# Attention and feed-forward on one core: 32-bit back transposes, a residual added by DMA, and a fifth shift tile

## The chip, the cores and the metric

The kernel runs on one core of one Trainium2 chip. The metric is the device time of one launch in microseconds (us), the median over runs. Engines are named as the profile names them: PE is TensorE (PEld its weight loads), DVE is VectorE, ACT is ScalarE, POOL is GpSimd, and SP is SyncE, which here only issues DMAs. PSUM has eight banks of 128 partitions by 512 fp32 numbers; matmuls write there, and ACT and DVE read it.

## The reference, cut to what matters

```python
x = A_x                                   # 2048 x 512, bf16
xn = _layernorm(x)
q = (xn @ wq) as 32 heads of 16;  k = xn @ wk;  v = xn @ wv     # one k and v for all heads
p = softmax(q k^T * 16 ** -0.5);  o = p v;  s = o @ wo
g = silu(silu(xn @ w1) @ w2)              # w1 512 x 1792, w2 1792 x 512
out = x + s * g
```

The exponentials are the largest part: 32 heads by 2048 queries by 2048 keys, which is 2048 tiles of 128 by 512.

## The kernel before, in words

**Units and groups.** The attention is cut into 32 groups of 64 units. A unit is one PSUM bank of scores (128 x 512), written by four 64x32 matmuls (`score`: L967 with a weight load, L961 where the weights that are loaded serve a second time). Its exponential is made in one of two ways. As a unit of kind A it goes to ACT, which takes one bank or two neighbouring banks in one instruction (`act_step`, L1674), and then into one product with the values. As a unit of kind D it goes to DVE, which in one pass (`pass_d`, L1042) writes an integer approximation of the exponential into `db_sb`; when a batch of eight such units is complete, POOL makes three shifted copies of it (`split`, L1225, `int64_add` on 4096 columns into a tile of `ds_sb`), and all four copies are multiplied with values of different weight and summed. So a D unit costs one DVE pass, three eighths of a POOL shift, and four products with the values where an A unit has one. Products with the values are line L1303 (`do_pv`).

**PE lanes.** Most matmuls are 64x32 tiles of the array. Four of them make up one half of the array, and two such halves, called lanes, run side by side: scores on lane 1, products with the values on lane 0, and the dense products (`product`, L705) on both.

**The rest of the work.** The layer norm runs ahead on DVE; `xn_sb` holds four normalised tiles, which PE transposes. For each quarter of the rows, `mk_h` and `mk_z` make the two feed-forward products; ACT and DVE apply the gates (`gated`, L761 and L762), and the gated result of a tile waits in `tmp_sb`. When a group is done (`make_norm`), DVE transposes its bank in 32x32 blocks (L1320), takes reciprocals (L1323) and multiplies into `otr_sb` (L1325); for every second group it transposes `otr_sb` back into `on_sb` (L1335), 512 bf16 columns. `mk_w` multiplies `on_sb` with wo for tiles 0 to 11; `final` then takes two DVE passes, bank times 0.25 times `tmp_sb` back into the bank (L814), and bank plus `xr_sb`, the reloaded x, into `ob_sb` (L817), which SP stores (L809). The last four tiles have a tail of their own (L1514 onward).

**The order.** Nothing is scheduled at run time. A planner in the file lays all operations out in a planned time, with a cost for each operation, and writes one fixed order per engine; each engine then runs its order and waits on semaphores. At each step PE's planner chooses between an A and a D unit by comparing the planned backlogs of ACT and of DVE:

```python
if a is not None and (d is None or ab < bl + mix.SLACK + mix.noise()):
```

so work moves between ACT and DVE until both are equally late. Thresholds such as `MARGIN` (a D batch is begun in a group only while at least so many of its units are unassigned) are drawn anew every 6000 planned ns from a list of seeds. The functions that the change and the prediction touch are these, as they stand before:

```python
NPA, NDB, NDS, NTM = 27, 3, 4, 4
MARGIN, MARGIN_END = 17, 20
...
def pick_d(t):
    if st["assigned"] < 8 or any(k not in evac_kt or evac_kt[k].op is None for k in range(NKT)):
        return None
```

The four tiles of `ds_sb` also hold x while it is normalised, in their last two; the first two are free for shifts from the start. The wait of `pick_d` is for the keys of all 16 tiles. POOL and DVE instructions that are marked `ports=2` are kept apart in the plan (`avail`).

Of the kernel before, what the change touches and what calls it, by code (L numbers as in the profile page):

```python
# [15 lines left out]
P = 128  # L16
# [6 lines left out]
SEEDS, STRETCH = [0, 0, 882634, 0, 348373, 328499, 78780, 554384, 89101, 903077, 320169, 0, 878569, 280070, 102111, 381856, 427096, 265022, 0, 740569, 0, 0, 0, 191854, 393933, 374197, 266972, 0, 665170, 0, 882882, 218695, 9227, 955074, 159633, 731624, 518155, 138034, 620799, 357599, 376984, 365473, 457970, 796664, 668429, 641664, 991272, 0, 0, 23990, 593814, 88565, 504692, 394759, 276845, 267858, 882770, 104810, 721623, 135503, 603776, 0, 337714, 100793, 638616, 0, 419715, 752789, 751312, 664693, 308960, 0, 762547, 276261, 218757, 897693, 0, 624478, 290921, 0, 713781, 335568, 417921, 100939, 814701, 0, 180062, 99721, 614963, 258262, 411291, 131548, 802432, 314922, 883804, 569039, 54637, 401726, 110613, 0, 983842, 914345, 0, 0, 0, 0, 0, 0, 0, 0], 6000.0  # L23
# [32 lines left out]
NPA, NDB, NDS, NTM = 27, 3, 4, 4  # L56
MARGIN, MARGIN_END = 17, 20
# [10 lines left out]
MATE = 176.663  # L68
RH, EVR, SC_PRIO, PES = 0, (0, 2, 3), 0, (1, 0)
# [6 lines left out]
class Task:  # L76
    __slots__ = ("eng", "dur", "emit", "reads", "writes", "prio", "preds", "op", "on_place", "dma", "gate", "ports", "after", "ring", "first")

    def __init__(self, eng, dur, emit, reads=(), writes=(), prio=5, preds=(), on_place=None, dma=0, gate=None, ports=1):
        self.ports, self.after, self.ring = ports, None, None  # L80
# [15 lines left out]
class Planner:  # L96

    def __init__(self):
# [7 lines left out]
        self.held = None  # L106
# [3 lines left out]
        self.last2 = {DV: None, PO: None}  # L110

# [68 lines left out]
    def tensor(self, mode, lane, dur, emit, reads, writes, t, after=None, n=8, held=None):  # L180
# [18 lines left out]
        if both or lane == 1:  # L199
            self.held = held  # L200
# [18 lines left out]
    def avail(self, task):  # L219
# [5 lines left out]
        if task.eng == PO and task.ports == 2:  # L225
            for d in self.tasks[DV]:
                if d.ports == 2 and d.gate is None and all(p.op is not None for p in d.preds) and (
                        self.ready(DV, d.reads, d.writes) <= self.clk[PO] + HOLD_PO):
                    return None
# [25 lines left out]
    def finalize(self, new_sem):  # L255
# [40 lines left out]
        for e in ENGINES:  # L296
            n = 0
            for op in self.order[e]:
# [5 lines left out]
                elif op.dma:  # L304
                    op.sem, op.val = new_sem(f"d{nd}"), 16
                    nd += 1
                elif op.inc:
                    n += 1
                    op.sem, op.val = sems[e], n

# [41 lines left out]
def bass_recurrent_scan__grouped_kv_mqa__dense_activation_silu__prompt_kernel(  # L352
# [29 lines left out]
    with ExitStack() as es:  # L382
# [25 lines left out]
        tmp_sb = sb("tmp_sb", [P, NTM, D], BF16)  # L408
        fin_sb = sb("fin_sb", [P, 2, D], BF16)
        ob_sb = sb("ob_sb", [P, 4, D], BF16)  # L410
        xr_sb = sb("xr_sb", [P, 4, D], BF16)
# [15 lines left out]
        pa3 = pa_sb[:].rearrange("p (b n) -> p b n", n=NQ)  # L427
        XB = NDS - 16 // BS
# [6 lines left out]

        pl = Planner()
        mix = Mix(A_HIGH=A_HIGH, D_HIGH=D_HIGH, SLACK=SLACK, MATE=MATE, HOLD=HOLD, PRESS=PRESS, PAIR_WAIT=PAIR_WAIT, STARVED=STARVED, SKIP=SKIP, J_SLIP=J_SLIP, START_H=START_H, START_Z=START_Z, JLATE=JLATE, NEXT_OB=NEXT_OB, OB_SLACK=OB_SLACK, MARGIN=MARGIN)
# [4 lines left out]
        xv = xf.rearrange("(t p) d -> p t d", p=P)  # L442

# [53 lines left out]
        pl.add(Task(PO, 1800.0, lambda g: g.memset(kt_sb[0:DH, 1, :], 0.0), [("xn", 3)], [("kt1", c) for c in range(NC)], 3,  # L497
                    gate=lambda: all(xn_task[t].op is not None for t in range(4)), ports=2))
        q1_fill = {}
        for r in range(NQR):  # L500
            q1_fill[r] = pl.add(Task(PO, T_MS, lambda g, r=r: g.memset(qt_sb[:, r, 1, :], 0.0), (), [("q1", r), ("qT", r, 1)], 2, ports=2,  # L501
# [1281 lines left out]
```

## Time and profile before

| | before |
|---|---|
| median of 3 runs | 658.18 us (658.02 to 658.38) |
| span of the profiled execution, first to last instruction | 656.6 us |
| its device time outside the span, by the median | 1.6 us |
| busy: PE, ACT, DVE, POOL | 648.1, 640.4, 639.3, 571.0 us |
| instructions | 44475 |
| granted TensorE clock | 1.000 |

The profiled execution has no time of its own beside its span, so the median stands for it. Busy time counts an engine that works on anything; PE's is no measure of its rate, since its matmuls overlap. In the groups of instructions the mean duration of one instruction is longer than the step from one to the next, since the start of one overlaps the end of the one before; where a step matters it is read from the timeline.

### The profile page before, as it was taken

To read this page: it belongs to the slowest core of one execution; us is meant where nothing else is said; L and a number is where in the kernel's file an instruction comes from. 1 tells how busy PE (TensorE), PEld (TensorE's weight loads), DVE (VectorE), ACT (ScalarE), POOL (GpSimd) and SP (SyncE) were. 2 spreads that over 40 slices of the span, in tenths; PEclk is the share of its full clock that TensorE was granted. 3 is DMA by queue.
4 is the path that set the end of the run, shared out by engine and by line. 5 is a ranking of instruction groups with operands and counts; after the bars stand their busy time and mean duration, and the time that the engine had idled before them with its cause. 6 is when DMAs were issued, how large, how long until landed. Compare 5 with 4: busy or idle time off the path is not lost.

```text
span 656.6 us, 44475 instructions
## 1 busy us (share of the span) xinstructions
PE 648.1 (99%) x22180; PEld 330.7 (50%) x19436; DVE 639.3 (97%) x1170; ACT 640.4 (98%) x1128; POOL 571.0 (87%) x320
## 2 busy tenths in 40 slices
PE   8999999999999999999999999999999999999997
PEld 4445554544455554554555454444555555554444
DVE  8999999999999999999999999999999999999976
ACT  6889999999999999999999999999999999999995
POOL 4038899999998978999999878999999999889991
PEclk9999999999999999999999999999999999999999
DMA  6311111000011100000000010000000000100001
GB/s 177 129 48 42 42 28 29 10 4 10 5 35 28 35 28 4 10 4 6 9 4 12 20 36 26 4 5 9 5 10 4 10 21 20 35 11 5 4 4 34
DMA packets 13641, 15.92 MB, mean 24 GB/s; under 512 B 2320, under 2 KB 12816, under 8 KB 13456
## 3 DMA queue, kind: packets, MB, share of 16 engines
q1 hardware_dynamic: 12976, 12.36, 6.3%
q8 instruction: 162, 2.65, 1.7%
q0 software_dynamic: 192, 0.46, 0.2%
q10 hardware_dynamic: 288, 0.26, 0.1%
q14 instruction: 23, 0.19, 0.1%
HBM read 8.95 MB, written 2.10 MB: 17 GB/s over the span
## 4 chain that ended last, share of the span: by engine, by line
PE 84%; ACT 10%; DVE 3%; POOL 1%; DMA 0%; issue 0%
PE ps L967 28%; PE ps L1303 23%; PE ps L705 20%; PE ps L961 13%; ACT pa_sb L1674 9%; ACT t_sb L761 1%; DVE stats_sb L539 1%; DVE xn_sb L568 1%; PE ps L1514 1%; DVE xnT_sb L618 0%; DMA kt_sb<-kt_sb 0%; POOL qt_sb L501 0%; POOL kt_sb L497 0%; DVE v_sb L679 0%; DVE kt_sb L651 0%
## 5 line engine op out<-in xcount | busy, mean ns | idle before, releaser
L1674 ACT ACTIVATE pa_sb<-ps 128x512 bf16<-128x512 f32 (+1 forms) x1038 | 611.0, 771 | 4.1 <-PE ps L967 3.8
L1225 POOL INT64_ADD ds_sb<-db_sb x300 | 562.1, 1896 | 41.5 <-DVE db_sb L1042 31.9
L1042 DVE TENSOR_SCALAR db_sb<-ps 128x512 uint16<-128x512 f32 x808 | 499.9, 680 | 4.2 <-PE ps L961 2.0
L967 PE MATMUL ps<-qt_sb,kt_sb 64*32 64x512 bf16 x5448 | 470.6, 378 | 1.5 <-DVE v_sb L679 0.8
L1303 PE MATMUL ps<-ds_sb,v_sb 64*32 64x512 bf16 x4848 | 350.5, 377 | 0.0
L1303 PE MATMUL ps<-pa_sb,v_sb 64*32 64x512 bf16 x2480 | 269.9, 377 | 0.5 <-DVE v_sb L679 0.5
L961 PE MATMUL ps<-qt_sb,kt_sb 64*32 64x512 bf16 x2744 | 263.6, 375 | 0.0
L967 PEld LDWEIGHTS ps<-qt_sb,kt_sb 64*32 64x32 bf16 x5448 | 130.4, 89 | 162.8 <-ACT pa_sb L1674 70.6
L1303 PE MATMUL ps<-db_sb,v_sb 64*32 64x512 bf16 x1616 | 210.6, 377 | 0.0
L1303 PEld LDWEIGHTS ps<-ds_sb,v_sb 64*32 64x32 bf16 x4848 | 133.4, 91 | 43.5 <-issue 15.0
L705 PE MATMUL ps<-xnT_sb,w_sb 64*32 64x512 bf16 x1792 | 134.6, 377 | 0.0
L705 PE MATMUL ps<-w_sb,u_sb 64*32 64x512 bf16 x1792 | 133.5, 376 | 0.0
L1303 PEld LDWEIGHTS ps<-pa_sb,v_sb 64*32 64x32 bf16 x2480 | 91.4, 91 | 26.8 <-issue 7.9
L1303 PEld LDWEIGHTS ps<-db_sb,v_sb 64*32 64x32 bf16 x1616 | 66.5, 91 | 15.7 <-issue 5.3
L705 PEld LDWEIGHTS ps<-xnT_sb,w_sb 64*32 64x32 bf16 x1792 | 42.8, 91 | 24.9 <-issue 6.7
L705 PEld LDWEIGHTS ps<-w_sb,u_sb 64*32 64x32 bf16 x1792 | 44.4, 91 | 20.3 <-issue 6.2
L761 ACT ACTIVATE t_sb<-ps 128x512 bf16<-128x512 f32 x72 | 49.1, 682 | 0.0
L762 DVE SCALAR_TENSOR_TENSOR u_sb<-t_sb,ps 128x512 bf16<-128x512 bf16 x56 | 37.9, 677 | 1.0 <-ACT t_sb L761 1.0
L705 PE MATMUL ps<-xnT_sb,wq_sb 64*32 64x512 bf16 x480 | 37.1, 377 | 0.0
L705 PE MATMUL ps<-wo_sb,on_sb 64*32 64x512 bf16 x384 | 30.2, 377 | 0.0
L1320 DVE STREAM_TRANSPOSE ps<-ps 128x512 f32<-128x512 f32 (+1 forms) x33 | 23.2, 706 | 3.6 <-PE ps L1303 3.6
L1349 POOL DMA_DIRECT2D kt_sb<-kt_sb x4 | 2.3, 566 | 21.3 <-DVE rstd_sb L559 7.8
(78 smaller groups left out, 193.0 us busy)
## 6 DMA issues: line engine op xcount, KB each, us to landing
xr_sb<-in_A_x_dram SPq DMA_DIRECT2D x16, 128.0 KB, 2.4
out_dram<-ob_sb SPq DMA_DIRECT2D x16, 128.0 KB, 1.8
w_sb<-in_B_w_dram SPq DMA_DIRECT2D x1, 1792.0 KB, 7.3
w_sb<-in_B_w_dram SPq DMA_DIRECT2D x14, 128.0 KB, 2.1
ds_sb<-in_A_x_dram SPq DMA_DIRECT2D x3, 512.0 KB, 7.1
qt_sb<-qt_sb SPq DMA_DIRECT2D x16, 96.0 KB, 2.2
wq_sb<-in_A_wq_dram SPq DMA_DIRECT2D x1, 512.0 KB, 5.4
wo_sb<-in_A_wo_dram SPq DMA_DIRECT2D x4, 128.0 KB, 2.9
```

The lines of the kernel that those rows point to most:

```text
L539: ts_ = pl.add(Task(DV, 593.0, lambda v, t=t: v.bn_stats(stats_sb[:, t, :], x_tile(t)), [xkey(t)], [("st", t)], 1 + j, gate=(lambda j=j: S ...
L568: xn_task[i] = pl.add(Task(DV, 323.0, lambda v, i=i: v.tensor_scalar(xn_sb[:, i % 4, :], x_tile(i), mv_sb[:, i, 0:1], rstd_sb[:, i:i + 1], ...
L705: h = pe.matmul(bank(b)[32 * j:32 * (j + 1), :], lhsT=lhs(k, rows, 32 * j, 32), rhs=rhs(k, rows), start=first, stop=last, tile_position=(r ...
L761: t1 = Task(AC, T_AF + 0.8333 * NQ, lambda a: a.activation(t_sb[:, k, :], bank(b), ACT.Tanh, scale=scale), [("ps", b)], [("t", k)], 0)
L762: t2 = Task(DV, T_P, lambda v: v.scalar_tensor_tensor(out=dst, in0=t_sb[:, k, :], scalar=1.0, in1=bank(b), op0=ALU.add, op1=ALU.mult), [(" ...
L961: h = pe.add_instruction(mybir.InstMatmult(name=pe.bass.get_next_instruction_name(), engine=mybir.EngineType.PE, ins=[pe.lower_ap(q), pe.l ...
L967: h = pe.matmul(to, lhsT=keys, rhs=q, start=True, stop=True, tile_position=(r0, 32 * j), skip_group_check=True)
L1042: bt.P[k] = pl.add(Task(DV, T_P, lambda v: v.tensor_scalar(db_sb[:, bt.b, k * NQ:(k + 1) * NQ], bank(b), 128.0 * LOG2E, 128.0 * (SHIFT_BET ...
L1225: whole["po"].append(pl.add(Task(PO, T_P64, lambda g: g.int64_add(ds_sb[:, s, :].bitcast(U64), db_sb[:, bt.b, :].bitcast(U64), words), rea ...
L1303: h = pe.matmul(bank(OB)[q:q + 32, :], lhsT=lhs[rows], rhs=rhs[rows], start=s0, stop=s1, tile_position=(64 * l, q), skip_group_check=True)
L1320: t1 = pl.add(Task(DV, (T_TR - 60.0) / parts + 60.0, lambda v, cols=cols: v.transpose(bank(OB)[:, cols], bank(OB)[:, cols]), [("ps", OB)], ...
L1674: op = pl.place(AC, 0.8333 * NQ * n + T_AF, lambda a: a.activation(pa3[:, k0:k1 + 1:max(1, k1 - k0), :], ps3[:, b0:b1 + 1:step, :], ACT.Ex ...
```

## The change

**Back transposes on 32-bit units.** `otr_sb` is written with two 32-column blocks interleaved, and the transpose into `on_sb` reads pairs of bf16 as one 32-bit word: 256 words in place of 512 elements. `on_sb` then holds the queries of a block pair alternately, and its readers take every second column.

```diff
+        def on_cols(slot, rows, q, n):
+            if not TR32:
+                return on_sb[rows, slot, q:q + n]
+            b = q // 64 * 64 + q % 64 // 32
+            return on_sb[rows, slot, b:b + 63:2]
...
+                    return v.tensor_tensor(
+                        o4[:, pairs, :, DH * e:DH * e + DH], f3[:, bl, 0:DH].rearrange("p (b s) d -> p b s d", s=2),
+                        rcp_sb[:, e, bl].rearrange("p (b s) -> p b s", s=2).unsqueeze(3).to_broadcast([P, nb // 2, 2, DH]), ALU.mult)
...
+                    on_sb[:, oi % NON, cols].bitcast(FP32), otr_sb[:, oi % 2, cols].bitcast(FP32)) if TR32 else v.transpose(
...
-            product(jb, lambda k, rows, a, n: on_sb[rows, (NOC * c + k) % NON, r * P + a:r * P + a + n],
+            product(jb, lambda k, rows, a, n: on_cols((NOC * c + k) % NON, rows, r * P + a, n),
```

**Residual of tiles 0 to 11 by accumulating DMAs.** SP copies each x tile into the output in DRAM during the second quarter. `final` is one DVE pass into `ob_sb`, and POOL issues a DMA that adds `ob_sb` to the output.

```diff
         def final(tt, b):
-            k = tt % 2
+            if tt < NT - 4:
+                t1 = Task(DV, T_P, lambda v: v.scalar_tensor_tensor(
+                    out=ob_sb[:, tt % 4, :], in0=bank(b), scalar=0.25, in1=tmp_sb[:, tt % NTM, :], op0=ALU.mult, op1=ALU.mult),
+                    [("ps", b), ("xn", tt % NTM)], [("ob", tt % 4)], 0, [tmp_task[tt], out_task.get(tt - 4)])
+                fin_task[tt] = t1
+                out_task[tt] = pl.add(Task(PO, T_SWDGE, lambda e: e.dma_start(ov[:, tt, :], ob_sb[:, tt % 4, :], accum_op=ALU.add),
+                                           [("ob", tt % 4)], [("out", tt)], 0, [t1, xr_task[tt]], dma=256 * 1024, on_place=outs.append))
+                return t1,
...
+            if tt < NT - 4:
+                xr_task[tt] = pl.add(Task(SP, 60.0, lambda e: e.dma_start(ov[:, tt, :], xv[:, tt, :]),
+                                          (), [("out", tt)], 2, [], dma=256 * 1024))
+                later(xr_task[tt], hidden(1, tt))
+                return
```

**Buffers.** `tmp_sb` becomes another name of `xn_sb`; the tail's x, `fin_sb` and a new `fx_sb` lie in w1's memory, written after w1's last reader. The memory that is freed holds a fifth shift tile, so that three are free from the start.

```diff
-NPA, NDB, NDS, NTM = 27, 3, 4, 4
-MARGIN, MARGIN_END = 17, 20
+NPA, NDB, NDS, NTM = 27, 3, 5, 4
+MARGIN, MARGIN_END = 24, 20
...
+        tmp_sb = xn_sb
+        late = w1_sb[:].rearrange("p c f -> p (c f)")[:, 0:10 * D].rearrange("p (k n) -> p k n", n=D)
+        xr_sb, fin_sb, fx_sb = late[:, 0:4, :], late[:, 4:6, :], late[:, 6:10, :]
```

**Thresholds and order.** D units may start when the keys of 12 tiles are there, behind the layer norm's own passes; two waiting D passes in neighbouring banks are made in one instruction; POOL's two-port instructions also wait for DVE's gated ones; and the list of seeds is another, so that the whole order is laid out anew. Further parameters come in with values that leave them without effect (products with the values on lane 1, zero fills and transposes by DMA).

```diff
+DPAIR, JA, JD = 25.0, 9000.0, 9000.0
+TR32, XBAR, T_TURN = 1, 0, 500.0
+YIELD, W_LATE = 1, 0.0
+DK, PRO_PRIO, ZDMA = 12, 6, 0
...
-            if st["assigned"] < 8 or any(k not in evac_kt or evac_kt[k].op is None for k in range(NKT)):
+            if st["assigned"] < 8 or any(k not in evac_kt or evac_kt[k].op is None for k in range(DK)):
...
-                op0=ALU.mult, op1=ALU.add), [("ps", b)], [("Db", bt.b, k)], 0, on_place=placed))
+                op0=ALU.mult, op1=ALU.add), [("ps", b)], [("Db", bt.b, k)], lambda: 0 if x_free[0] else PRO_PRIO, on_place=placed))
+            bt.P[k].slot = (b, bt.b * BS + k)
...
+        def both_passes(t, one):
+            for two in pl.tasks[DV]:
...
+                r = pl.avail(two)
+                if r is None or r > t + mix.DPAIR:
+                    continue
+                (b0, k0), (b1, k1) = sorted((one.slot, two.slot))
+                if k0 > k1 or b1 != b0 + 1:
+                    continue
...
+                op = pl.place(DV, one.dur + NQ / 0.96, lambda v: v.tensor_scalar(
+                    db3[:, k0:k1 + 1:k1 - k0, :], ps3[:, b0:b1 + 1:b1 - b0, :], 128.0 * LOG2E, 128.0 * (SHIFT_BETA + 127.0),
```

More of the change, by code (lines that the diff above doesn't have):

```diff
@@ L198, in tensor @@
         op.lane, op.n = lane, n
-        if both or lane == 1:
-            self.held = held
+        for i in range(2):
+            if both or i == lane:
+                self.helds[i] = held
         for i in range(2):
@@ L1305, in emit @@
                 return h
-            pl.tensor("U", 0, MM, emit, sorted(reads, key=str), [("ps", OB)], t, n=4 * len(mm))
+            last = ob_last.get(g)
+            ob_last[g] = pl.tensor("U", lane, MM, emit, sorted(reads, key=str), [("ps", OB)], t, n=4 * len(mm),
+                                   after=last if last is not None and last.lane != lane else None)
             make_shifts()
```

213 lines of the change are left out of this document (147 added, 66 removed).

## The prediction

> **What bounds the kernel now.** I read the page first (who is busy), then the windows between the first and the last shift on POOL (who is never idle), then the waits, and last the timeline for the step of each operation.
>
> ```profile
> PE 648.1 (99%) x22180; PEld 330.7 (50%) x19436; DVE 639.3 (97%) x1170; ACT 640.4 (98%) x1128; POOL 571.0 (87%) x320
> ```
> ```profile
> 0.00:44.80 44.80, 40.43 (x968) 19.35 (x882) 39.74 (x137) 35.74 (x63) 8.95 (x21) 1.00 0.41 128
> 44.80:642.70 597.90, 597.78 (x21000) 306.33 (x18352) 591.17 (x1017) 597.80 (x1057) 562.05 (x300) 1.00 0.06 16
> 642.70:656.60 13.90, 9.86 (x240) 4.98 (x212) 8.36 (x18) 6.84 (x11) 0.00 (x0) 1.00 0.12 40
> ```
> ```profile
> 625.48 0.39 PE L967 MATMUL ps<-qt_sb,kt_sb 64*32 64x512 bf16 x4
> ...
> 626.12 0.39 PE L967 MATMUL ps<-qt_sb,kt_sb 64*32 64x512 bf16 x4
> ```
> ```profile
> PEld ps L967 <- ACT pa_sb L1674: 70.6, 292, 0.5
> PEld ps L967 <- DVE db_sb L1042: 35.7, 165, 0.4
> POOL ds_sb L1225 <- DVE db_sb L1042: 31.9, 25, 5.7
> ...
> PEld ps L1303 <- POOL ds_sb L1225: 2.3, 8, 0.4
> ```
>
> The columns of the windows are length, PE, PEld, DVE, ACT, POOL. In the 597.9 us of the middle ACT is idle for 0.1 us and DVE for 6.7. PE's busy time says nothing, its count does: three score steps lie 0.64 us apart, so a lane makes four matmuls in 0.213 us and both lanes eight. The 21000 matmuls need 21000 / 8 x 0.213 = 559 us, so PE has 39 us to spare. POOL is idle for 35.9 us and mostly waits for DVE. The waits agree: the scores' weight loads stand 70.6 + 35.7 = 106 us for a bank that ACT or DVE still reads, and next to nothing waits for POOL. So ACT and DVE bound the middle together, and since the planner moves units between them, work taken off DVE is shared: a unit moved from A to D costs DVE one pass and saves ACT one exponential.
>
> ```profile
> L1674 ACT ACTIVATE pa_sb<-ps 128x512 bf16<-128x512 f32 x836 | 446.2, 694 | 2.6 <-PE ps L967 2.4
> L1674 ACT ACTIVATE pa_sb<-ps 128x1024 bf16<-128x1024 f32 x202 | 213.7, 1090 | 1.5 <-PE ps L967 1.4
> L817 DVE TENSOR_TENSOR ob_sb<-ps,xr_sb 128x512 bf16<-128x512 f32 x12 | 8.1, 677 | 0.0
> L814 DVE SCALAR_TENSOR_TENSOR ps<-ps,tmp_sb 128x512 f32<-128x512 f32 x12 | 8.2, 686 | 0.0
> L803 DVE SCALAR_TENSOR_TENSOR fin_sb<-ps,tmp_sb 128x512 bf16<-128x512 f32 x1 | 0.7, 692 | 1.1 <-PE ps L591 1.1
> L1335 DVE STREAM_TRANSPOSE on_sb<-otr_sb 128x512 bf16<-128x512 bf16 x15 | 10.5, 702 | 0.0
> L1320 DVE STREAM_TRANSPOSE ps<-ps 128x512 f32<-128x512 f32 x31 | 22.4, 723 | 2.1 <-PE ps L1303 2.1
> L1320 DVE STREAM_TRANSPOSE ps<-ps 128x256 f32<-128x256 f32 x2 | 0.8, 444 | 1.5 <-PE ps L1303 1.5
> L1325 DVE TENSOR_TENSOR otr_sb<-ps,rcp_sb 128x256 bf16<-128x256 f32 x31 | 12.7, 409 | 0.0
> L1325 DVE TENSOR_TENSOR otr_sb<-ps,rcp_sb 128x128 bf16<-128x128 f32 x2 | 0.4, 263 | 0.0
> L1349 POOL DMA_DIRECT2D kt_sb<-kt_sb x4 | 2.3, 566 | 21.3 <-DVE rstd_sb L559 7.8 <-DVE kt_sb L651 7.4 <-DVE mv_sb L543 6.1
> L705 PEld LDWEIGHTS ps<-wo_sb,on_sb 64*32 64x32 bf16 x384 | 8.9, 91 | 6.5 <-DVE db_sb L1042 1.4 <-issue 1.1 <-PE ps L705 0.7
> ```
> ```profile
> 39.20 3.67 DVE L1042 TENSOR_SCALAR db_sb<-ps 128x512 uint16<-128x512 f32 x6
> ...
> 74.58 0.70 DVE L1335 STREAM_TRANSPOSE on_sb<-otr_sb 128x512 bf16<-128x512 bf16 x1
> 75.21 2.45 DVE L1042 TENSOR_SCALAR db_sb<-ps 128x512 uint16<-128x512 f32 x4
> ...
> 208.44 0.67 DVE L817 TENSOR_TENSOR ob_sb<-ps,xr_sb 128x512 bf16<-128x512 f32 x1
> 209.03 0.24 DVE L1323 RECIPROCAL rcp_sb<-ps 128x16 f32<-128x16 f32 x1
> ...
> 649.26 0.76 DVE L1335 STREAM_TRANSPOSE on_sb<-otr_sb 128x256 bf16<-128x256 bf16 x2
> ```
> ```profile
> 47.63 0.49 ACT t_sb L761
> ```
>
> **The residual.** Twelve passes L817 go, none comes for them. In the timeline it starts at 208.44 and the next instruction at 209.03: a step of 0.59 us, and 12 x 0.59 = 7.1 us off DVE. The other pass now writes bf16 into SBUF where it wrote fp32 into PSUM: the same form in the tail (L803) lasts 692 ns against 686, so nothing. POOL gains twelve DMA issues. An accumulating DMA isn't in this trace; the nearest row is POOL's plain DMA (566 ns), and the next is a shift, 562.05 / 300 = 1.87 us. I take 0.57, the same kind of instruction, 6.8 us in all, hidden in POOL's 35.9 us of idle time. If POOL had no room, each microsecond more on it would come back as moved units, which is the rival on POOL below. The new wait: POOL waits for `final`'s pass, with the next shifts queued behind it, and PE's products behind those; the plan puts the issue where the pass has ended, and 2.3 us of PE's waits on POOL are the present scale.
>
> ```profile
> SPq L715 <- DVE qt_sb L723: 260.5, 14, 40.2
> ```
> ```profile
> DMA  6311111000011100000000010000000000100001
> ```
>
> SP loses twelve stores and keeps twelve x transfers, now from DRAM to DRAM. SP runs in order and stands up to 40 us before a move of queries, but these transfers have no consumer except the accumulation, and the moves that are queued behind them wait for DVE, not for SP. The DMA engines are busy for one or two tenths of a slice after the opening. `final` waits for the accumulation four tiles earlier to leave its buffer, a quarter of the kernel before. Zero for all three.
>
> **The back transposes.** Now 512 elements in 702 ns, with a step of 75.21 - 74.58 = 0.63 us. 32-bit transposes are in the trace at L1320: 512 words take 723 ns, the same as 512 short elements, and 256 words take 444. So the count sets the time, and the saving is 0.702 - 0.444 = 0.26 us, 15 x 0.26 = 3.9 us off DVE. The two halves in the tail (0.76 us together) lose the time of 128 elements each; by L1320's slope, (723 - 444) / 256 = 1.09 ns, that is 0.14 us each, and they lie in the tail's chain: 0.2 us off the end, since part of the second overlaps. The price: L1325 now writes every second bf16. Its slope is (409 - 263) / 128 = 1.14 ns an element. If a scattered write ran at half rate, 31 x 256 x 1.14 = 9.0 us would come onto DVE; below nothing it can't go, as the count stays. No row has a scattered write of this kind. [...] PE's weight loads of `on_sb` read every second column; the row now is 91 ns and overlaps the matmuls, and PE has its 39 us. Zero, and at double duration 384 x 91 ns / 4 = 8.7 us, still inside them (four loads run together).
>
> **Paired passes.**
>
> ```profile
> L1042 DVE TENSOR_SCALAR db_sb<-ps 128x512 uint16<-128x512 f32 x808 | 499.9, 680 | 4.2 <-PE ps L961 2.0 <-PE ps L967 1.1 <-POOL ds_sb L1225 0.2
> L651 DVE TENSOR_SCALAR kt_sb<-ps,part_sb 128x512 bf16<-128x512 f32 x3 | 2.2, 731 | 0.0
> L651 DVE TENSOR_SCALAR kt_sb<-ps,part_sb 128x384 bf16<-128x384 f32 x1 | 0.6, 600 | 0.0
> ```
>
> Six passes in a row take 3.67 us, the last of them its full 0.68, so the step of a pass is (3.67 - 0.68) / 5 = 0.60 us. A second bank in one instruction adds its 512 elements, 0.56 us by L1320's slope and 0.52 by L651's, (731 - 600) / 128 = 1.02 ns. So a pair saves 0.04 to 0.08; I take 0.06. How many? ACT, whose planner looks for neighbours, has 202 pairs. DVE's planner takes only those that happen to be ready within 25 ns, in neighbouring banks, in the right order, while PE stands 35.7 us for banks of DVE, so scores start one by one as banks come free. I take 20, between 0 and 135 (ACT's share, 404 of 1240 units, of some 820), 1.2 us. [...]
>
> **The sum for the middle.** DVE loses 7.1 + 3.9 + 1.2 = 12.2 us. A moved unit costs DVE 0.60 us and saves ACT 0.49 (the chain's step of one bank). Both end together when 12.2 - 0.60 n = 0.49 n, so n = 11.2 units and the gain is 5.5 us. What those units bring: 11.2 x 3 more products of two matmuls, 67 matmuls, 1.8 us of PE's 39; 11.2 x 3/8 = 4.2 shifts, 7.9 us of POOL. With the issues POOL takes 14.7 us more, and its room is 35.9 - 5.5 = 30.4. Both are covered. If no unit moved, ACT would still end where it does and the gain would be nothing: that is the lower bound.
>
> **The opening, the fifth tile, the rest.** Before 44.8 us ACT idles 9.1 us and DVE 5.1. D units may start with 12 tiles' keys, and three shift tiles stand free, but DVE has the layer norm to finish, and passes go behind it. If three or four of them fit in DVE's gaps, 2.1 us x 0.49 / 1.09 = 1.0 us; the bounds are 0 and 2.3 (all 5.1 us). The fifth tile and the higher `MARGIN` give POOL more room, where nothing waits: zero.
>
> ```profile
> L568 DVE TENSOR_SCALAR xn_sb<-ds_sb,mv_sb,rstd_sb x16: 403/408/415, 7.2 to 33.8; 128x512 bf16<-128x512 bf16 x16
> L762 DVE SCALAR_TENSOR_TENSOR tmp_sb<-t_sb,ps x16: 629/679/689, 119.3 to 634.2; 128x512 bf16<-128x512 bf16 x16
> L705 PE MATMUL ps<-xnT_sb,w_sb x1792: 373/376/388, 26.0 to 567.4; 64*32 64x512 bf16 x200
> L1514 PE MATMUL ps<-wo_sb,on_sb x96: 376/376/387, 645.4 to 650.1; 64*32 64x512 bf16 x96
> ```
>
> The columns here are shortest, median and longest duration, and first and last start. `xn_sb` is written last at 33.8 us and takes its new tenant at 119.3; w1 is read last at 567.4, and the tail's products with wo, which come before its x is needed, start at 645.4. So the shared buffers add waits that are over before they begin: zero. A newly drawn order may be a little better or worse everywhere; no row prices that, and I give it 2 us to either side, about the ends of the opening's bounds.
>
> Span: 656.6 - 5.5 - 0.2 - 1.0 = 649.9. The median lies 1.6 us above the profiled span, so 651.5 us.
>
> **The rivals.**
> - *More than the balance.* The opening is filled better (half of ACT's 9.1 us: 4.5 x 0.60 / 1.09 = 2.5, in place of 1.0) and pairs are as frequent as ACT's, 135 (115 more x 0.06 x 0.45 = 3.1). 646.9 us. For it: ACT's idle time is there. Against: DVE is the late one in the opening.
> - *The scattered write costs.* L1325 at half rate gives 9.0 of the 12.2 us back: 3.2 x 0.45 = 1.4 in place of 5.5, so 655.6 us. For it: no row excludes it. [...]
> - *Slower: pairs hold banks.* A pair frees its first bank 0.52 us later than a single pass, and PE already waits for DVE's banks 165 times in 808 passes. If each pair stops the score lane that long, and the other lane goes on, half of it counts: at 200 pairs 200 x 0.26 = 52 us, of which PE has 39 - 1.8 = 37 to spare; 15 are left, less 180 x 0.06 x 0.45 = 4.9 that the pairs save DVE: 661.6 us. The spare time is used up from 142 pairs, and the present time is passed from some 185. For it: PE waits for banks more than for anything else. Against: few passes can meet the condition.
> - *Slower: POOL becomes the bound.* The room for the issues, 30.4 - 7.9 = 22.5 us, is used up at 1.87 us each. At twice a shift, 3.75 us, the excess is 22.5 us, and a unit given back frees 3/8 x 1.87 = 0.70 us of POOL for 0.49 on ACT: 22.5 / 1.19 x 0.49 = 9.3, so 660.8 us; the present time is passed from 3.2 us an issue. Against: the four plain issues take 0.57 us, though beside few DVE passes. [...]
> - *It isn't what it says*: no unit moves, the order alone is new: about 658 us.
>
> **How the numbers follow.** Forecast 0.64 (649 to 655 with the 2 us of order and the bounds of the opening, of it 0.02 within 0.2% and 0.03 slower, if the new order is a bad one), more than the balance 0.13, scattered write 0.07 (0.02 of it within 0.2%), held banks 0.08, POOL 0.06 (0.02 within), order alone 0.02 (within). The range 646.5 to 658.5 takes in all but the held banks, most of POOL and the edges. A measurement of this kernel tells 0.2% (1.3 us) from no change. Faster by more: 0.59 + 0.13 + 0.05 = 0.77; within: 0.02 + 0.02 + 0.02 + 0.02 = 0.08; slower: 0.03 + 0.08 + 0.04 = 0.15.
>
> **What would show it.** L817 gone; L1335 at 256 words near 0.44 us; L1325 still 409 ns; some 819 D units (passes L1042, pairs counted twice) where there were 808, and 304 shifts on POOL; POOL's new DMA near 0.6 us; ACT idle under 1 us in the middle, which is 5.5 us shorter. Wrong it is if the D units don't rise, if a wait of ACT on PE or of PE on POOL grows by over 5 us, or if pairs exceed a hundred.

## The result and the profile after

| | before | after |
|---|---|---|
| median of 20 runs each, in alternation | 658.17 us | 659.21 us |
| ratio of after to before, 95% interval | | 1.0016 [1.0009, 1.0022] |
| span of the profiled execution | 656.6 us | 657.4 us |
| units of kind A, of kind D | 1240, 808 | 1232, 816 |
| paired passes on DVE, paired exponentials on ACT | 0, 202 | 2, 191 |

The change makes the kernel slower by 1.0 us. The interval of the ratio lies above 1, but the difference is inside the 0.2% that count as no change. The forecast was 651.5 us, the range ended at 658.5. The busy times of the page of after, in the order of the first line that was shown of before:

```profile
PE 648.3 (99%) x22227; PEld 333.7 (51%) x19696; DVE 639.5 (97%) x1168; ACT 637.4 (97%) x1131; POOL 579.2 (88%) x331
```

DVE, from which 12 us were to be taken, is as busy as before (639.5 against 639.3). ACT has lost 3.0 us, and the span has grown by 0.8. The windows say where. Both kernels are cut at the same times, first before, then after; the columns are length, PE, PEld, DVE, ACT, POOL:

```profile
0.00:41.00 41.00, 36.63 (x852) 17.65 (x780) 35.94 (x131) 31.94 (x57) 8.92 (x20) 1.00 0.45 138
41.00:640.00 599.00, 598.88 (x21020) 306.33 (x18380) 592.44 (x1020) 598.90 (x1058) 559.39 (x299) 1.00 0.06 16
640.00:665.00 25.00, 12.56 (x324) 6.67 (x284) 10.89 (x22) 9.54 (x15) 2.68 (x2) 0.98 0.07 23
```
```profile
0.00:41.00 41.00, 36.21 (x870) 18.06 (x818) 38.42 (x135) 29.98 (x54) 8.96 (x20) 1.00 0.44 138
41.00:640.00 599.00, 598.89 (x21048) 309.59 (x18594) 590.80 (x1014) 598.89 (x1065) 570.11 (x311) 1.00 0.07 16
640.00:665.00 25.00, 13.23 (x331) 6.00 (x300) 10.26 (x22) 8.53 (x14) 0.08 (x1) 0.95 0.07 23
```

ACT is never idle in the middle of either kernel, so a span is ACT's busy time plus its idle time at the two ends. In the opening ACT is idle for 41 - 31.94 = 9.1 us before and 11.0 after, which is 2.0 more (31.94 - 29.98). From 640 us to the end of the span it is idle for 16.6 - 9.54 = 7.1 and 17.4 - 8.53 = 8.9 us, which is 1.8 more. Together: -3.0 + 2.0 + 1.8 = +0.8, as measured. The forecast took 5.5 us of work off ACT in the middle and 1.0 by D units that begin in the opening, together 6.5 where ACT's busy time fell by 3.0; it left ACT's idle time in the opening as it was, and took 0.2 us off the tail. So the 7.5 us between forecast and result are 3.5 of work that stayed on ACT, 2.0 of idle time in the opening and 2.0 in the tail.

The idle time that ACT gained at the two ends is waiting for PE. Its waits for scores, first before and then after, all of them in the opening:

```profile
ACT pa_sb L1674 <- PE ps L967: 3.8, 5, 1.1
```
```profile
ACT pa_sb L1780 <- PE ps L1024: 5.7, 9, 1.3
```

In the tail it waits once for the dense products, 3.9 us before and 5.7 after (both lines are shown further down). That makes 1.9 + 1.8 = 3.7 us more, of the 3.8 us of added idle time.

The groups of instructions of after, by form, that answer to the prediction's:

```profile
L1102 DVE TENSOR_SCALAR db_sb<-ps 128x512 uint16<-128x512 f32 x812 | 504.4, 680 | 4.5 <-POOL ds_sb L1289 2.6 <-PE ps L1371 0.2
L1809 DVE TENSOR_SCALAR db_sb<-ps 128x1024 uint16<-128x1024 f32 x2 | 2.5, 1226 | 0.7 <-POOL ds_sb L1289 0.7
L855 DVE SCALAR_TENSOR_TENSOR ob_sb<-ps,xn_sb 128x512 bf16<-128x512 f32 x12 | 8.1, 675 | 0.0
L1413 DVE STREAM_TRANSPOSE on_sb<-otr_sb 128x256 f32<-128x256 f32 x15 | 6.5, 435 | 0.0
L1413 DVE STREAM_TRANSPOSE on_sb<-otr_sb 128x128 f32<-128x128 f32 x2 | 0.5, 286 | 0.0
L1402 DVE TENSOR_TENSOR otr_sb<-ps,rcp_sb 128x256 bf16<-128x256 f32 x31 | 13.7, 442 | 0.1
L1285 DVE TENSOR_SCALAR ds_sb<-db_sb 128x4096 uint16<-128x4096 uint16 x7 | 8.3, 1221 | 0.1
L1289 POOL INT64_ADD ds_sb<-db_sb x299 | 562.9, 1946 | 31.1 <-PE ps L1371 13.7 <-DVE db_sb L1102 9.6 <-DVE ds_sb L1285 5.6
L859 POOL DMA_DIRECT2D out_dram<-ob_sb x12 | 11.0, 914 | 0.6 <-DVE ob_sb L855 0.2 <-issue 0.2
L1780 ACT ACTIVATE pa_sb<-ps 128x512 bf16<-128x512 f32 x850 | 450.7, 700 | 6.0 <-PE ps L1024 5.7
L1780 ACT ACTIVATE pa_sb<-ps 128x1024 bf16<-128x1024 f32 x191 | 200.3, 1095 | 0.1
```

The same group on DVE's shifts in before, from its last 57 us:

```profile
L1221 DVE TENSOR_SCALAR ds_sb<-db_sb 128x4096 uint16<-128x4096 uint16 x3 | 3.5, 1222 | 0.0
```

This is DVE's account, in busy time. The residual pass has gone (-8.1), and the transposes are shorter (10.5 to 6.5, and 0.2 in the halves). In their place stand the passes of eight more D units (499.9 to 504.4 + 2.5, +7.0), seven shifts where there were three (3.5 to 8.3, +4.8), and a dearer scattered write (12.7 to 13.7, +1.0). The sum is +0.5, and 0.2 was measured. The shifts of both engines together rose by three, from 303 to 306, which is what eight D units need; but DVE makes four more of them and POOL one fewer.

The waits of after, in us in total, times, and the longest:

```profile
PEld ps L1024 <- ACT pa_sb L1780: 65.2, 278, 0.4
PEld ps L1024 <- DVE db_sb L1102: 42.0, 194, 0.4
PEld ps L1371 <- issue: 32.0, 138, 0.4
POOL ds_sb L1289 <- PE ps L1371: 13.7, 15, 2.1
...
POOL ds_sb L1289 <- DVE db_sb L1102: 9.6, 10, 3.3
```

The scores wait for banks for 65.2 + 42.0 = 107 us, as before (106), only less for ACT and more for DVE. POOL waits less for DVE (9.6 against 31.9); a fifth tile and earlier batches would do that, but no run took them away. PE waits for POOL's shifts no longer than before (1.9 us against 2.3), so this gains nothing.

### The profile page after: what moved, and what is told of

It is laid out like the page before. It is cut to its first block, busy times and chain, and to the rows that moved or that the text cites. A ratio compares the mean times of both kernels' runs of the same rounds, so it can differ in the third digit from the quotient of the medians.

```text
span 657.4 us, 44814 instructions
## 1 busy us (share of the span) xinstructions
PE 648.3 (99%) x22227; PEld 333.7 (51%) x19696; DVE 639.5 (97%) x1168; ACT 637.4 (97%) x1131; POOL 579.2 (88%) x331
## 4 chain that ended last, share of the span: by engine, by line
PE 88%; DVE 9%; POOL 1%; issue 0%
PE ps L1024 29%; PE ps L1371 25%; PE ps L746 19%; PE ps L1018 13%; DVE db_sb L1102 4%; DVE stats_sb L571 1%; POOL ds_sb L1289 1%; DVE u_sb L803 1%; DVE xn_sb L600 1%; PE ps L1593 1%; DVE xnT_sb L650 0%; PE ps L639 0%; DVE v_sb L720 0%; DVE var_sb L594 0%; DVE var_sb L596 0%
## 5 line engine op out<-in xcount | busy, mean ns | idle before, releaser
L1289 POOL INT64_ADD ds_sb<-db_sb x299 | 562.9, 1946 | 31.1 <-PE ps L1371 13.7
L1102 DVE TENSOR_SCALAR db_sb<-ps 128x512 uint16<-128x512 f32 x812 | 504.4, 680 | 4.5 <-POOL ds_sb L1289 2.6
L1024 PE MATMUL ps<-qt_sb,kt_sb 64*32 64x512 bf16 x5660 | 478.5, 378 | 1.4 <-DVE v_sb L720 1.0
L1371 PE MATMUL ps<-ds_sb,v_sb 64*32 64x512 bf16 x4896 | 356.2, 377 | 0.0
L1371 PE MATMUL ps<-pa_sb,v_sb 64*32 64x512 bf16 x2464 | 257.7, 377 | 0.4 <-DVE v_sb L720 0.4
L1018 PE MATMUL ps<-qt_sb,kt_sb 64*32 64x512 bf16 x2532 | 243.5, 375 | 0.4 <-DMA qt_sb<-qt_sb 0.3
L1024 PEld LDWEIGHTS ps<-qt_sb,kt_sb 64*32 64x32 bf16 x5660 | 135.6, 89 | 167.7 <-ACT pa_sb L1780 65.2
L1371 PE MATMUL ps<-db_sb,v_sb 64*32 64x512 bf16 x1632 | 187.0, 377 | 0.0
L1371 PEld LDWEIGHTS ps<-ds_sb,v_sb 64*32 64x32 bf16 x4896 | 134.2, 91 | 37.6 <-issue 14.1
L746 PE MATMUL ps<-xnT_sb,w_sb 64*32 64x512 bf16 x1792 | 136.1, 377 | 0.0
L1371 PEld LDWEIGHTS ps<-pa_sb,v_sb 64*32 64x32 bf16 x2464 | 86.5, 91 | 25.4 <-issue 10.7
L1371 PEld LDWEIGHTS ps<-db_sb,v_sb 64*32 64x32 bf16 x1632 | 59.6, 91 | 15.9 <-issue 7.2
```

Of the source, the lines that this page charges most:

```text
L746: h = pe.matmul(bank(b)[32 * j:32 * (j + 1), :], lhsT=lhs(k, rows, 32 * j, 32), rhs=rhs(k, rows), start=first, stop=last, tile_position=(r ...
L1018: h = pe.add_instruction(mybir.InstMatmult(name=pe.bass.get_next_instruction_name(), engine=mybir.EngineType.PE, ins=[pe.lower_ap(q), pe.l ...
L1024: h = pe.matmul(to, lhsT=keys, rhs=q, start=True, stop=True, tile_position=(r0, 32 * j), skip_group_check=True)
L1102: bt.P[k] = pl.add(Task(DV, T_P, lambda v: v.tensor_scalar(db_sb[:, bt.b, k * NQ:(k + 1) * NQ], bank(b), 128.0 * LOG2E, 128.0 * (SHIFT_BET ...
L1289: whole["po"].append(pl.add(Task(PO, T_P64, lambda g: g.int64_add(ds_sb[:, s, :].bitcast(U64), db_sb[:, bt.b, :].bitcast(U64), words), rea ...
L1371: h = pe.matmul(bank(OB)[q:q + 32, :], lhsT=lhs[rows], rhs=rhs[rows], start=s0, stop=s1, tile_position=(64 * l, q), skip_group_check=True)
```

## The experiments

Each kernel ran in alternation with the kernel before, on the same chip, and its ratio is to that. After itself stands at 1.0016. One thousandth is 0.66 us.

**Theories.** (T1) No engine alone bounds the kernel: PE, ACT and DVE are late together in the order that is written down, and work taken from one of them buys next to nothing. (T2) DVE's relief is worth its exchange for units, as forecast, but something the change adds eats it: the opening, the DMAs, four more shifts, or the newly drawn order.

### The two savings alone, in the order of before

Both kernels keep the order of before, instruction by instruction. The transposes go on 32-bit units, L814 writes `ob_sb` directly, and L817 shrinks to 8 columns: in the first kernel as an addition of two tiles of SBUF, in the second as a fill. Both leave out the residual x of tiles 0 to 11, and no DMA adds it.

```diff
-                out=bank(b), in0=bank(b), scalar=0.25, in1=tmp_sb[...], op0=ALU.mult, op1=ALU.mult),
+                out=ob_sb[:, tt % 4, :], in0=bank(b), scalar=0.25, in1=tmp_sb[...], op0=ALU.mult, op1=ALU.mult),
...
-            t2 = Task(DV, T_P, lambda v: v.tensor_tensor(ob_sb[:, tt % 4, :], bank(b), xr_sb[:, tt % 4, :], ALU.add),
+            t2 = Task(DV, T_P, lambda v: v.tensor_tensor(ob_sb[..., 0:8], ob_sb[..., 0:8], xr_sb[..., 0:8], ALU.add),   # the first kernel
+            t2 = Task(DV, T_P, lambda v: v.memset(ob_sb[:, tt % 4, 0:8], 0.0),                                          # the second
```

> The order of before, instruction for instruction, with both reliefs put in place: back transposes on 32-bit units, and in final one full pass into ob_sb and the second pass cut to 8 columns (it leaves out the residual x in the other columns of tiles 0 to 11, and adds no DMA). DVE loses some 4 us at the transposes and 6 at the second pass, less 1 at L1325's scattered write: busy about 630 us. Theory O (ACT sets the middle, relief pays only where units move): at most 1 us faster, 657 to 658. Rival R (DVE's own lateness sets the end): up to 5 us faster, 653 to 655.

> The order of before with both reliefs in place, as tried already, but final's second pass is now a memset of 8 columns, which reads nothing (it leaves out the residual of tiles 0 to 11, and loses those 8 columns). DVE loses 4 us at the transposes and some 6 at final, less 1 at the scattered write: busy about 630. Theory C: within 1.5 us of before. If the earlier 5 us of loss came from the two-input pass of 8 columns, which took 0.96 us beside POOL's shifts, the loss is gone; if it came from the 32-bit transposes or the strided weights in before's order, it stays at 3 us or more.

The first gave 1.0068 [1.0051, 1.0086], the second 1.0001 [0.9991, 1.0010]. Their rows of the shrunken pass, the first kernel's and then the second's:

```profile
L821 DVE TENSOR_TENSOR ob_sb<-ob_sb,xr_sb 128x8 bf16<-128x8 bf16 x12 | 11.6, 964 | 0.0
```
```profile
L821 DVE MEMSET ob_sb<- 128x4 uint32 x12 | 0.7, 62 | 0.0
```

The first kernel is no test of the relief. Eight columns took 964 ns where 512 columns from PSUM had taken 677, so its DVE got no relief at all (busy 640.3 us). Its rows spread from 157 to 1770 ns, about a POOL shift at the top, and the same instruction on 512 columns takes 424 ns in the tail, where POOL has finished; that it waits for the shifts is read from these numbers, and was not tried by itself. The second kernel is the clean one. DVE's busy time fell by 7.1 us to 632.2, and nothing came of it:

```profile
PE 647.7 (99%) x22179; PEld 330.9 (50%) x19436; DVE 632.2 (96%) x1170; ACT 640.1 (98%) x1128; POOL 570.7 (87%) x320
```

In a fixed order a DVE that is 7 us lighter is worth nothing here, since ACT works without a pause as before. The prediction had this as its lower bound, for no unit moved; so this run does not tell what the relief is worth where units can move.

### The order

Without the seed list the thresholds stay at their base values; that was run with either kernel, each with its own (`MARGIN` is 17 before and 24 after). The third kernel is after with its own order, but with the transposes on 16-bit units again.

```diff
-SEEDS, STRETCH = [0, 0, 882634, ...], 6000.0        # before; 761112, ... in after
+SEEDS, STRETCH = [], 6000.0
```
```diff
-TR32, XBAR, T_TURN = 1, 0, 500.0
+TR32, XBAR, T_TURN = 0, 0, 500.0
```

> The kernel before with an empty list of seeds, so that every stretch of the order is laid out with the base thresholds. Theory O (the order decides: the list of seeds is worth as much as the whole change): 3 to 5 us above before, 661 to 663 us. Theory P (POOL bounds the changed kernel, seeds are noise): within 1.5 us of before.

> The changed kernel with an empty list of seeds. Theory O: 662 to 665 us, and within 2 us of the kernel before without seeds, so that the seeds of both are worth several us and the change little at equal thresholds. Theory P: at 659 to 660 us, as with its seeds, since POOL sets the time.

> The changed kernel's order, instruction for instruction, with the back transposes on 16-bit units again: DVE gets 15 x 0.27 = 4 us back, less 1 at L1402. Theory O: the relief lies in gaps of DVE's order, so at most 1.5 us slower, 659 to 661. Rival R: DVE is tight, 3 us slower or more, 662 up.

Without the list, before stands at 1.0054 [1.0039, 1.0069] and after at 1.0123 [1.0108, 1.0138]. So the list is worth 0.0054, or 3.6 us, to before, and 0.0107, or 7.0 us, to after. At base thresholds the changed kernel is 1.0123 / 1.0054 = 1.0069, or 4.5 us slower. The list belongs to the change, and what it adds over the old list hides 3.5 us of that. Neither theory had after without its list so slow: 662 to 665 us were expected, within 2 us of before without a list, and it took 666.9. After with the slow transposes stands at 1.0066 [1.0049, 1.0082], 3.3 us above after, and DVE's busy time is 642.8, 3.3 us above it. Theory O allowed 1.5 us and missed. So DVE's time is not worthless: in an order planned with short transposes their return is paid in full. Taking DVE work out of an order (the experiment above) gave nothing, and putting work in costs all of it, as if each order were fitted to its own durations.

Of T2 one part holds so far: the order decides more than the savings.

### Which engine bounds it

These kernels are after with its order untouched, and one engine made lighter at regular intervals, by leaving out half the columns of some of its instructions: busy time falls by 8.9 us on ACT, 11.9 on DVE and, in the run with all four lighter, 17.5 on POOL, less than the 20 that the expectations say; on PE the halved matmuls are worth an estimated 19 us, worked out from their count (some 350) and the 0.213 us of four matmuls.

```diff
+                w = NQ // 2 if st["nx"] > 100 and st["nx"] % 12 == 0 else NQ
-                    pa3[..., :], ps3[..., :], ACT.Exp),
+                    pa3[..., 0:w], ps3[..., 0:w], ACT.Exp),
```

That is the edit for ACT. For DVE every 8th pass after the 200th, for PE every 6th product with the values after the 100th, and for POOL every 13th shift is halved in the same way.

> The changed kernel's order, instruction for instruction; every twelfth exponential instruction on ACT after the hundredth covers only half its columns (the other half keeps old numbers), some 78 instructions, about 20 us off ACT spread over the run. Theory A (ACT alone sets the middle, as the prediction has it): 8 to 15 us faster than the changed kernel, 644 to 651. Theory C (ACT, DVE and PE are coupled through eight banks in a fixed order, so relief of one alone finds the others late): at most 4 us faster, 655 to 659.

> The same order; every eighth D pass on DVE after the two hundredth covers half its columns, some 76 passes, 20 us off DVE. Theory A: at most 1 us faster. Theory C: at most 4 us faster, 655 to 659. Theory D (DVE is the late one, as 16-bit transposes in the same order cost about what they add): 8 us or more faster.

> The same order; every sixth product with the values, neither first nor last of a group, covers half its columns, some 350 products on one lane, 19 us of the pair of lanes off PE. Theory A and D: at most 1 us. Theory E (PE's order is the late one, as its 88% of the chain says): 5 us or more faster. Theory C: 1 to 4 us.

> The same order; every thirteenth shift on POOL is cut to half its columns, some 21 shifts, 20 us off POOL. Theory P (POOL, without a gap from 120 to 340 us, holds the changed kernel): 5 us or more faster. Theories A, C and D: at most 1.5 us.

| lighter | ratio to before, interval | against after |
|---|---|---|
| ACT | 0.9990 [0.9981, 0.9999] | -1.7 us |
| DVE | 1.0022 [1.0013, 1.0032] | +0.4 us |
| PE | 1.0014 [1.0005, 1.0024] | -0.1 us |
| POOL | 1.0028 [1.0018, 1.0037] | +0.8 us |

Only ACT's relief shows, and the gain is a fifth of the 8.9 us. The three others bring nothing. The middle of the run with the lighter ACT, in the same columns as above:

```profile
41.00:640.00 599.00, 598.89 (x21108) 337.03 (x18644) 591.31 (x1017) 592.06 (x1068) 569.69 (x311) 1.00 0.07 16
```

ACT now pauses for 6.9 us there, where it had paused for 0.1. Where the profile names what ended a pause before an exponential, it is PE (22 pauses in the whole run, 8.7 us). The chain of work that ended last, by engine, in after, in the run with the lighter ACT and in the run with the lighter PE:

```profile
PE 88%; DVE 9%; POOL 1%; issue 0%
```
```profile
PE 93%; DVE 6%; issue 0%; DVEq 0%
```
```profile
PE 54%; ACT 30%; DVE 11%; POOL 3%; issue 1%; DVEq 0%
```

PE carries most of the chain already in after, and nearly all of it with ACT lighter; with PE lighter, ACT and DVE come into it. The waits of the scores' weight loads for banks say the same. The run with the lighter PE, and then that with ACT and DVE lighter, whose time is in the second table:

```profile
PEld ps L1024 <- ACT pa_sb L1783: 94.3, 365, 0.5
PEld ps L1024 <- DVE db_sb L1102: 54.7, 241, 0.5
```
```profile
PEld ps L1024 <- DVE db_sb L1104: 28.4, 128, 0.3
PEld ps L1024 <- ACT pa_sb L1784: 22.7, 106, 0.4
```

A lighter PE waits 149 us for banks in place of 107, so it spends what it saves on waiting. With ACT and DVE lighter the waits fall to 51 us, yet the time by no more than 2.3. If the three are late together, reliefs must add up only when they come together:

> The changed kernel's order with both reliefs of before together: every twelfth exponential on ACT and every eighth pass on DVE at half its columns, 20 us off each. Theory C (ACT, DVE and PE are late together, so PE's 0.95 of its rate is the next limit): 3 to 7 us faster than the changed kernel. Theory A/D (ACT and DVE alone share the bound, PE has 39 us to spare, as the prediction has it): 12 us or more faster.

> The same order with ACT's 20 us and PE's 19 us off, DVE as it is. Theory C: 2 to 5 us faster, DVE being the late one. Theory A: as with ACT alone, within 1 us of it.

> The same order with 20 us off ACT, 20 off DVE and 19 off PE. Theory C: 10 to 18 us faster than the changed kernel, as no engine is left late. Rival F (a fixed order doesn't pay for relief at all, since its waits are laid out for other durations): at most 5 us faster.

> The changed kernel with all four reliefs: every 12th exponential after the 100th, every 8th pass after the 200th and every 6th product of the values after the 100th work on half of their columns, and every 13th shift of GpSimd after the 24th on half of its words (left out: those columns, about 20 us per engine; the order of the instructions is unchanged). The first three alone gave 0.9933, 5.5 us below the changed kernel. If GpSimd is the fourth of the engines that are late together, the ratio falls to 0.985 to 0.989 (another 3 to 5 us). If the rest is held by the fixed order and by the parts that the reliefs don't touch (the first 40 us, the tail, the units that are not shortened), it stays at 0.991 to 0.994.

| lighter | ratio to before, interval | against after |
|---|---|---|
| ACT and DVE | 0.9981 [0.9971, 0.9990] | -2.3 us |
| ACT and PE | 0.9982 [0.9972, 0.9991] | -2.2 us |
| ACT, DVE and PE | 0.9933 [0.9918, 0.9948] | -5.5 us |
| these and POOL | 0.9935 [0.9921, 0.9948] | -5.3 us |

```profile
PE 642.8 (99%) x22227; PEld 330.4 (51%) x19696; DVE 624.8 (96%) x1168; ACT 626.7 (96%) x1131; POOL 578.3 (89%) x331
```

These busy times are of the run with three reliefs. One engine buys at most 1.7 us, the two pairs that were tried (DVE with PE was not) 2.3 and 2.2, and three 5.5, which is more than the sum of the three alone. PE's relief, worth nothing alone, brings 3.2 us on top of the other two (by the two intervals some 1.2 us either way). So T1 holds in kind: PE, ACT and DVE are late together. POOL is not among them: its relief adds nothing to the other three.

In size T1 was not met. Theory C had 1 to 4 us for PE alone, where nothing came, 3 to 7 for ACT and DVE, where 2.3 came, and 10 to 18 for all three, where 5.5 came. Theory A, by which ACT, or ACT and DVE, set the time and PE has room, is refuted (8 to 15 and 12 or more were expected). Rival F, by which a fixed order pays for hardly any relief, had at most 5 us for all three, and 5.5 cannot be told from that; what it does not explain is that PE's relief pays only beside the others. Even with three reliefs the time falls by about half of what ACT's busy time lost (10.7 us) and a third of what DVE's did (14.7). The rest is held by what was not touched, the fixed order, the opening and the tail; between these the runs do not tell. The tests leave the order as it is. How much a relief would be worth in an order drawn anew for it stays open, except for the one case that is the change itself.

### The opening and the last group

Two settings of the change act at one place each. The first kernel returns to the old rule for the first passes on DVE, the second takes all shifts of the last group off DVE.

```diff
-DK, PRO_PRIO, ZDMA = 12, 6, 0
+DK, PRO_PRIO, ZDMA = 16, 0, 0
```
```diff
-CLOSING, URGENT, END_DV = 0, 4.336, 58
+CLOSING, URGENT, END_DV = 0, 4.336, 0
```

> The changed kernel with the base's rule for VectorE's first passes (DK = 16 and PRO_PRIO = 0: none before all 16 tiles' keys are evacuated, and none behind the opening's work). The order behind it is planned anew, and the seed list no longer fits it, so the total may rise by several us for that alone (the planner's own end is 4 us later); the window of the first 41 us is what is read. If the early passes cause ScalarE's 1.9 us of added idle time, its busy time in the first 41 us goes back from 30.0 to about 32 us and the first pass from 32.9 to about 39 us. If the order of the other opening work causes it, ScalarE's busy time in that window stays at 30 to 30.5 us. Total: ratio 1.004 to 1.010.

> The changed kernel with END_DV = 0: VectorE takes no shift in the last group any more, so its seven there (1221 ns each, 8.5 us) go back to GpSimd. If the engines are late together and VectorE alone is not the bound (the reading so far), VectorE's busy time falls from 639.5 to about 631-632 us and the ratio stays within 0.999 to 1.003, that is at the changed kernel's 1.0016 within about 1 us. If the four added shifts of the last group were where the relief was lost, the time falls by 3 to 5 us (ratio 0.994 to 0.997). If the shifts were put on VectorE because GpSimd is late there, the products wait for GpSimd at the end and the time rises by 2 to 8 us (ratio 1.005 to 1.014), with GpSimd still busy after 640 us.

The old rule gave 1.0079 [1.0067, 1.0091], 4.1 us above after: as with the empty list, the rest of the order is another. Its opening:

```profile
0.00:41.00 41.00, 36.51 (x854) 18.17 (x818) 37.18 (x133) 30.47 (x57) 8.97 (x20) 1.00 0.45 139
```

The first pass moved from 32.9 to 38.0 us, and ACT gained 0.5 of the 2.0 us. So the early passes do not cause most of that loss. It begins before them, as the timeline of ACT shows, first before and then after (start, length, and at the end the pause ahead of it):

```profile
19.70 6.04 ACT L1674 ACTIVATE pa_sb<-ps 128x512 bf16<-128x512 f32 x11
26.45 4.14 ACT L1674 ACTIVATE pa_sb<-ps 128x1024 bf16<-128x1024 f32 x7 [0.71 <-PE ps L967]
```
```profile
20.00 1.51 ACT L1780 ACTIVATE pa_sb<-ps 128x512 bf16<-128x512 f32 x2
22.02 3.96 ACT L1780 ACTIVATE pa_sb<-ps 128x512 bf16<-128x512 f32 x7 [0.50 <-PE ps L1024]
26.52 2.06 ACT L1780 ACTIVATE pa_sb<-ps 128x512 bf16<-128x512 f32 x4 [0.55 <-PE ps L1024]
28.94 0.60 ACT L1780 ACTIVATE pa_sb<-ps 128x512 bf16<-128x512 f32 x1 [0.35 <-PE ps L1024]
```

Between 20 and 30 us ACT runs short of scores in after, while the first D pass is still to come. The traces point at PE's order: between 11 and 30 us PE runs 124 matmuls for scores in after and 148 before, but 192 for the projection of the values (L711) and 136 before (L670). The kernel with the old rule has the same 124 and 192, which fits that the old rule did not give the time back. That these products hold up the scores is read from the counts; no run moved them.

Without DVE's shifts in the last group the ratio is 1.0025 [1.0016, 1.0035], 0.6 us above after, and DVE's busy time is 631.0, 8.5 us less. DVE has its relief and the kernel is no faster. POOL, which takes the work over, is busy for 8.2 us after 640 us, where it was for 0.1, so this run cannot say what the shifts would be worth if nobody had to make them; the run with the lighter DVE, whose halved passes reach into the last group, says that in this order DVE's time is worth nothing there either.

## Why the prediction was wrong

**What was right.** L817 is gone. The 32-bit transposes take 435 ns (444 said), and the two halves in the tail 286 each. L855 costs no more than L814. The accumulating DMAs are hidden: POOL waits 0.2 us for L855, and nobody waits for L859. The late buffers and the x transfers cost nothing that shows in the waits. PE waits for POOL no longer than before (1.9 us against 2.3), DVE a little (3.3 against 0.2). The scattered write stands in the sum at nothing, a term that no run shows: it took 33 ns more on 409, 1.0 us in all. That is far from the bound of 9.0 and refutes that rival; with two pairs the rival of held banks had no occasion; and POOL, which was not missed even with its work halved in places, is not the bound. The time came out nearest to the rival "the order alone" (about 658 us), but that is luck: by it no unit moves, and eight moved.

**The step that failed: "PE has 39 us to spare".** By this the prediction put PE at nothing and added up ACT and DVE alone. The 39 us came from a count, 21000 matmuls in steps of 0.64 us for three. The runs showed two things in its place. With ACT and DVE lighter, a lighter PE brought 3.2 us more (5.5 against 2.3), where an engine with 39 us of room should have brought next to nothing; and by itself it bought nothing. That is how a third co-bound engine looks. And in after itself ACT waits 3.7 us longer for PE at the two ends, where the prediction had no such wait grow. A count does not say whether the room lies where it is wanted: PE works in a fixed order, and a score that waits for its bank holds up what is queued behind it. This last is a reading; no run tried it alone.

**The sum for ACT's work.** PE is not what is missing here, for ACT pauses only 0.1 us in the middle of after. The forecast was 11.2 moved units for 5.5 us, and 1.0 us more from the opening; eight units moved, and ACT's busy time fell by 3.0. The step that failed in this term is that all of DVE's freed time goes into units. Four more shifts, which the prediction left to POOL, and the dearer write took 5.8 of the 12.2 us, and 1.1 us that 18 more pairs were to save never came. That leaves 12.2 - 1.1 - 5.8 = 5.3 us; with the 2.1 us of DVE's gaps in the opening, the prediction's own exchange gives 6.8 units and 3.3 us. So the exchange itself was about right, and what it was fed was too much. Whether the 5.8 us would have bought units is open: the run with the lighter DVE and the one without DVE's shifts gained nothing, but in neither could units move.

**The opening.** The early passes came as forecast: eight D passes begin in the first 41 us where four did, and DVE is busy there for 2.5 us more (2.1 were said). But ACT, which the prediction took to be untouched, was idle for 2.0 us more, waiting for PE's scores, and made 40 exponential instructions there where it had made 43. The early passes explain 0.5 of the 2.0.

**The tail.** ACT's exponentials end 1.0 us earlier than before, at 645.97 against 646.99 us, and the kernel 0.8 us later. ACT then waits for PE, first before and then after:

```profile
650.87 1.57 ACT L798 ACTIVATE xn_sb<-ps 128x512 bf16<-128x512 f32 x3 [3.88 <-PE ps L591]
```
```profile
651.70 1.58 ACT L839 ACTIVATE w_sb<-ps 128x512 bf16<-128x512 f32 x3 [5.73 <-PE ps L623]
```

So what ACT had gained by then PE did not pass on. The chain shows where PE was: the last products with the values (L1303, now L1371) and behind them the products with wo (L1514, now L1593), before and then after:

```profile
647.90 2.59 PE ps L1514 x68
```
```profile
647.91 0.82 PE ps L1371 x16
648.73 2.59 PE ps L1593 x48
```

The products with the values end at 648.73 us where they ended at 647.90, and what follows takes as long as before: this is the 0.8 us. From 640 us on PE has 164 of these matmuls left, where it had 148. That the added D units, with four products each, are what leaves it more stands to reason, but no run took only these away.

**Sizes.** Paired passes were put at 20 and are 2; that is 1.1 us of DVE time. A DMA issue on POOL was put at 0.57 us and takes 0.91; 4.1 us of POOL, hidden. The order was given 2 us to either side. Its list alone is worth 3.6 us to before and 7.0 to after, so this term should have been the widest of all, and with such a spread the range would have reached above the time before.

**The DMA issues and the pairs.** The issue of an accumulating DMA took 791 to 1172 ns beside DVE passes from PSUM, where the rival on POOL needed more than 3.2 us to pass the present time. The data landed 3.2 us after the issue (the median of 2.8 to 4.0), and no run has such a DMA without DVE beside it, so a delay behind the issue is not excluded. The pair took 1226 ns against 680 for one pass, so its second bank costs 0.55 us. With a step of 0.60 for a single pass, a pair saves 0.05 us, between the rows' 0.04 and 0.08, though on two instructions only.

## What to carry to other kernels

Where three in-order engines are each busy for 97% of the time or more, take no relief of one at its exchange rate: lighten each engine in turn in the unchanged order, then pairs and triples, and read from that which of them are late together. A fixed order is a part of the kernel's time like any instruction (3.6 and 7.0 us here), so a change that redraws it needs a spread of that size in its forecast, to both sides. And spare time that comes from a count of instructions is a guess until it is tested: PE's 39 us did not show when ACT and DVE were made lighter. Last, where the planner may put freed time to several uses, price them all; here shifts took what was meant for units.

## What the runs showed of the hardware

- An addition of two SBUF tiles on DVE took 964 ns in the mean for 8 columns beside POOL's shifts (157 to 1770), and 424 ns for 512 columns after POOL had ended. In after POOL waits three times for DVE's own shifts (5.6 us, on a semaphore), and some of its shifts are recorded at up to 2483 ns, where before none took longer than 1927; what makes them longer was not tried.
- DVE's transposes went by the count of elements, not by their bytes: 512 of 16 bits took 702 ns, 512 of 32 bits 723, and 256 of 32 bits, the same data as the first, 435.
- A DVE write to every second bf16 column took 8% longer (442 against 409 ns) with a source of fp32 in PSUM. In after with the 16-bit transposes the same product writes contiguously again and takes 414 ns.
- An accumulating DMA of 128 KB from SBUF to DRAM kept POOL for 0.91 us and landed 3.2 us after its issue.
